# Keeping a block's query weights and a quarter of a K tile on chip, with five stream slots instead of six

## The chip, the cores and the metric

The kernel runs on one core of a Trainium2 chip. The metric is the time of one execution on the device in microseconds. The kernel before takes 1979.28 us, the median of 3 runs (1979.23 to 1979.42).

## The reference

One token goes through four attention layers: block A, block B, block A again, block B again, with the same weights and caches the second time. Each block has 32 heads, a cache of 8192 keys and values of 192 numbers per head, and a model width of 640.

```python
def block(x, k_cache, v_cache, wq, wo):          # x (1, 1, 640)
    q = (x @ wq).reshape(1, 1, 32, 192).transpose(0, 2, 1, 3)
    scores = jnp.einsum("bhqd,bhkd->bhqk", q, k_cache) * (192 ** -0.5)
    o = jnp.einsum("bhqk,bhkd->bhqd", softmax(scores), v_cache)
    return o.transpose(0, 2, 1, 3).reshape(1, 1, 32 * 192) @ wo

x = x + block(layernorm(x), A_k, A_v, A_wq, A_wo)
x = x + block(layernorm(x), B_k, B_v, B_wq, B_wo)
x = x + block(layernorm(x), A_k, A_v, A_wq, A_wo)
x = x + block(layernorm(x), B_k, B_v, B_wq, B_wo)
```

All inputs are bf16. Each cache holds 32 x 8192 x 192 numbers, 100.7 MB, so four layers read some 805 MB of keys and values unless a part of them is kept on chip.

## The kernel before

**Tiles and slots.** Layers count from 0 to 3; layers 0 and 2 use block A's tensors, layers 1 and 3 block B's. Heads are worked on in 16 pairs. A pair's K tile, and likewise its V tile, is 6144 KB: 128 partitions, 64 of them for each head, with 48 KB each. It is handled as two halves of 3072 KB, u = 0 and 1. On chip there is a pool of eight slots of 3072 KB (`NSLOT`, `TS`), each with a semaphore of its own (`semS`). Everything that is streamed passes through these slots: K tiles, V tiles, the query weights `wq` (7680 KB, two and a half slots) and the output weights `wo` in three parts a layer.

**One pair.** `products` lets DVE multiply the K tile by the broadcast query, in place, and PE sum the products by matmuls with an identity matrix (24 of them per half). `softmax` reduces and exponentiates, `values` multiplies the weights with the V tile on PE, `gather` picks out and stores the pair's output. The half u of a K tile is free again when its 24 matmuls are done, a V tile when its values are. After five pairs, `columns` and `project_row` or `project` bring the outputs through `wo`.

**Queries.** Layer l needs its whole query before it can work on more than one pair. The first pair's query comes from matmuls with a broadcast left side (L529), the others from `q_rows` (60 matmuls into one row each, which ScalarE then scales) and `q_spread` (one matmul per pair that broadcasts the row). In layers 0 and 1 the whole `wq` is loaded; the columns of the pair that comes first in layer l + 2 are copied to `wq0` by DVE (L522), so that the later layer loads only the other 15 pairs' columns, 7200 KB.

**What stays.** `KEPT` names the tiles that are loaded in layers 0 and 1 and still there two layers later: K tile 0 of block A (its products in layer 0 go to two other slots, steps `t`) and V tiles 14 and 15 of block B. Through layers 0 and 1 six slots are left for the stream, in layer 2 four once K tile 0 is used up.

**The queue.** SP issues all transfers in the order of `plan`. `allot` gives each transfer slots when the kernel is built: those that come free first. `before` lists what must be done with them, `freed` the events, `transfer` issues after a wait for these events. SP works strictly in order, so a transfer that waits for its slot holds up all behind it. A tile whose halves lie in neighbouring slots is loaded by one transfer (`whole`), which then needs both slots free and lands as a whole. In layers 0 and 1 this holds for K except pairs 5 and 10, and for V except the last.

**Between layers 1 and 2.** At the end of layer 1 four slots hold V tiles 14 and 15 and two hold K tile 0 of block A. In one of the other two lies the last part of `wo`. Layer 2 loads its query weights in five rows of 1440 KB (`r`, L405): two into the free slot, the third when a part of `wo` has been used (`woa`), the fourth when the projection has ended, the fifth when the first has been used. Meanwhile `quarter` works on K tile 0 in four pieces, and the slot halves that they release take the first V tile (`vh`, L426).

The places to have at hand: L405 issues the rows of query weights, L430 and L432 whole and half tiles, L434 the whole `wq`, L443 `wo`; L563 and L72 are matmuls of the query rows (L72 is a helper that also serves products and values); L675 and L705 are DVE's products; L690, L714 and L72 PE's sums; L645 ends the projection of layer 0.

Of the kernel before, what the change touches and what calls it, by code (L numbers as in the profile page):

```python
# [77 lines left out]
PAIRS_W = 5  # L78
NSLOT = 8
KEPT = {0: {("k", 0)}, 1: {("v", 14), ("v", 15)}}  # L80


def build(nc, A_x, A_k, A_v, A_wq, A_wo, B_x, B_k, B_v, B_wq, B_wo, out):
# [13 lines left out]
    QC = (NPAIR - 1) * PD  # L97
    QR = QC // 3
# [13 lines left out]
    with ExitStack() as ctx:  # L112
# [12 lines left out]
        wq0 = [sb(f"wq0{i}", [P, DC, PD], BF16) for i in range(2)]  # L125
# [103 lines left out]
        def whole(kind, l, p):  # L229

            if kind == "t":
                return False
            if kind == "k":
                return l < 2 and p not in (PAIRS_W, 2 * PAIRS_W) or l == 3 and p > 1
            if p == NPAIR - 1:
                return False
            return l != 2 or p not in (0, PAIRS_W, 2 * PAIRS_W)

        steps, plan = [], []
# [5 lines left out]
        for l in range(NL):  # L245
            if l < 2:
                plan.append(("wq", l, 0))
                steps += [("wq", l, g) for g in range(3)]
            elif l == 2:
                plan += [("wq", l, g) for g in range(3)]  # L250
                steps.append(("r", l, 0))
            else:
                both(("wq", l, 0))
            for p in range(NPAIR):
                if first_load("k", l, p) == (l, p):
                    plan += [("k", l, p, u) for u in range(2)]
                if stays("k", l, p):
                    plan += [("t", l, p, u) for u in range(2)]
                if l == 2 and p == 0:
                    for i, q in enumerate(("mr", "md", "mdrr", "mdd")):  # L260
                        for c in q:
                            steps.append({"m": ("mq", l, p, i), "r": ("r", l, sum(n[:2] == ("r", l) for n in steps)),
                                          "d": ("rd", l, p, sum(n[:2] == ("rd", l) for n in steps))}[c])
                        if i == 1:
                            steps.append(("r", l, 2))
                else:
                    steps.append(("m", l, p, 0))
                    if l == 2 and p == 1:
                        steps.append(("e", l, 0))
                    steps.append(("m", l, p, 1))  # L270
# [5 lines left out]
                if p < NPAIR - 2:  # L276
                    if first_load("v", l, p) == (l, p):
                        plan += [("v", l, p, u) for u in range(2)]
                        if l == 2 and p == 1:
                            i = plan.index(("k", l, 1, 0))  # L280
                            plan[i - 1:i + 1] = [("k", l, 1, 0), ("v", l, 0, 1)]
# [25 lines left out]
        def released(n):  # L307

            if n[0] in "kvt":
                l, p = n[1:3]  # L310
                if n[0] != "t" and stays(*n[:3]):
                    l, p = l + 2, ORDER[l + 2]["pairs"].index(pair(l, p))
                return at[("v", l, p, 1) if n[0] == "v" and p == NPAIR - 1 else ("v", l, p) if n[0] == "v" else
                          ("mq", l, p, 2 * n[3] + 1) if (l, p) == (2, 0) else ("m", l, p, n[3])]
            return at[("wol", n[1]) if n[0] == "wo" and n[2] == 2 and NB[n[1]] else ("r", 2, (0, 3, 4)[n[2]]) if n[:2] == ("wq", 2) else n]

        place, before, holder = {}, {}, [None] * NSLOT

        def allot(n):

            if n[0] == "wq" and n[1] < 2:
                ns = [("wq", n[1], g) for g in range(3)]
            elif n[0] == "v" and (n[2] < NPAIR - 1 or n[1] == 1) or n[0] == "k" and whole(*n[:3]):
                ns = [n[:3] + (u,) for u in range(2)]
            else:
                ns = [n]
            k = len(ns)
            end = [-1 if h is None else released(h) for h in holder]
            first = -1 if n[1] == 0 and n[0] == "k" and stays(*n[:3]) else 1
            i = min(range(0, NSLOT - k + 1, 2 if k == 2 else 1), key=lambda i: (max(end[i:i + k]), first * i))  # L330
            if n[:3] == ("v", 2, 0):
                i = place["k", 0, 0, 0]
            for j, m in enumerate(ns):
                place[m] = i + j
                before[m] = [h for h in holder[i:i + k] if h is not None]
                if n[0] in "kv" and not whole(*n[:3]):
                    before[m] = [h for h in holder[i + j:i + j + 1] if h is not None]
            for j, m in enumerate(ns):
                holder[i + j] = m

        for n in plan:
            if n[0] == "wol":
                before[n] = [] if NB[n[1]] else [("wc", n[1], 2)]
            elif n[0] in ("wob", "vq", "woe"):
                before[n] = []
            elif n not in place:
                allot(n)
        assert before["wq", 2, 1] == [("wo", 1, 2)] and before["wq", 2, 2] == [("wq", 2, 0)] and before["v", 2, 0, 0] == [("k", 0, 0, 0)]
        for g, (c0, k) in enumerate(Q_PARTS):
            i = plan.index(("wq", 2, g))  # L350
            plan[i:i + 1] = [("r", 2, c) for c in range(c0, c0 + k)]
            for c in range(c0, c0 + k):
                before["r", 2, c] = before["wq", 2, g]
        before["r", 2, 2], before["r", 2, 4], before["vh", 2, 0] = [("woa", 1, 2)], [("r", 2, 0)], [("kq", 2, 0, 0)]
        plan.insert(plan.index(("v", 2, 0, 0)), ("vh", 2, 0))
        turn = {}
        for i, n in list(enumerate(plan)):
            if n[0] == "v" and n[3] == 0:
                m = n[:3] + (1,)
                turn[n[1:3]] = (0, 1)  # L360
                if n[2] < NPAIR - 1 and not whole(*n[:3]) and max(map(released, before[n])) > max(map(released, before[m])):
# [6 lines left out]
        def wq_rows(l, g):  # L368

            c0, k = Q_PARTS[g]  # L370
            if l < 2:
                i = place[("wq", l, 0)] * TS
                return pool[:, i + c0 * QW:i + (c0 + k) * QW].rearrange("p (c n) -> p c n", c=k)
            return slot[place[("wq", l, g)]][:, 0:k * QC].rearrange("p (c n) -> p c n", c=k)
# [8 lines left out]
        def transfer(n):  # L383
# [10 lines left out]
            if n[0] == "t":  # L394
                return max(free, key=lambda e: e[1]) if free else None
# [6 lines left out]
            if n[0] == "r":  # L402
                g = n[2] // 2
                i = place["wq", 2, g]
                return SP.op(lambda s: s.dma_start(  # L405
                    wq_rows(l, g)[:, n[2] % 2, :],
                    w["wq"][:, o["q1"] * PD:o["q1"] * PD + QC].rearrange("(p c) n -> p c n", c=DC)[:, n[2], :]), *free,
                    sem=semR[g] if n[2] % 2 else semS[i], inc=16)
            if n[0] == "vq":
                n = ("v", l, NPAIR - 1, 1)  # L410
            first = n[0] == "vh"
            if first:
                n = ("v", l, 0, 0)
            i = place[n]
            t = slot[i]
            if n[0] in "kv":
# [7 lines left out]
                if n == ("v", 2, 0, 0):  # L424
                    x = slice(0, TS // 2) if first else slice(TS // 2, TS)
                    return SP.op(lambda s: s.dma_start(t[:, x], r[:, x]), *free, sem=semS[i], inc=16)  # L426
                if whole(*n[:3]):
                    if n[3] == 1:
                        return landed[n[:3] + (0,)]
                    f = lambda s: s.dma_start(pool[:, i * TS:(i + 2) * TS], r)  # L430
# [4 lines left out]
            elif n[0] == "wq":  # L435
# [3 lines left out]
                    w["wq"][:, o["q1"] * PD:o["q1"] * PD + QC].rearrange("(p c) n -> p c n", c=DC)[:, c0:c0 + k, :])  # L439
# [59 lines left out]
        def layer(l, ev_z, ev_true):  # L499
# [17 lines left out]
            PE.wait(ev_xb, last["QB"])  # L517
            if l < 2:
                e = need(("wq", l, 0))
                every = pool[:, place[("wq", l, 0)] * TS:][:, 0:DC * QW].rearrange("p (c n) -> p c n", c=DC)  # L520
                q0 = ORDER[l + 2]["q0"] * PD
                ev_first[l] = DV.op(lambda v: v.tensor_copy(wq0[l][:], every[:, :, q0:q0 + PD]), e)  # L522
                q_first = every[:, :, ORDER[l]["q0"] * PD:(ORDER[l]["q0"] + 1) * PD]
            else:
                e = ev_first[l - 2]
                q_first = wq0[l - 2]
            PE.wait(e)
            for c in range(DC):
                e = PE.op(lambda t, c=c: t.matmul(  # L529
                    QM[:, 0:PD], lhsT=xb[:, c:c + 1].broadcast_to([P, P]), rhs=q_first[:, c, :],  # L530
                    start=(c == 0), stop=(c == DC - 1)), signal=(c == DC - 1), bank=QMu)
# [13 lines left out]
            q_halves(0, e, ev_rs, scale=rs)  # L545

            def q_rows(g, r0=0, r1=None):
# [3 lines left out]
                t3 = wq_rows(l, g)[:, :, ORDER[l]["q1"] * PD if l < 2 else 0:]  # L551
                PE.wait(need(("wq", l, 0)) if l < 2 else need(("r", 2, c0 + r0) if l == 2 else n), ev_xb, last["O"],
                        last["YB"], ev_first.get(l))
                r1 = k if r1 is None else r1
                for c in range(r0, r1):
                    for b in range(4):
                        w = min(512, QR - b * 512)
                        for r in range(3):
                            fin = c0 + c == DC - 1
                            o, x, y = (OY[32 * r:32 * r + 1, b * 512:b * 512 + w], xb[:, c0 + c:c0 + c + 1],  # L560
# [399 lines left out]
```

## Time and profile before

| | |
|---|---|
| median of 3 runs | 1979.28 us |
| span of the profiled execution | 1977.8 us |
| read from HBM | 848.36 MB, 429 GB/s over the span |
| PE busy | 1267.5 us (64%) |
| DVE busy | 1198.7 us (61%) |
| ACT busy | 168.2 us (9%) |
| chain that ended last | DMA 58%, PE 25%, DVE 15% |
| DVE products L675 | 360 of 2392 ns mean, idle before them 151.0 us, released by DMA |
| layer 2's query weights | 5 transfers of 1440 KB |
| layer 3's query weights | 2 of 2880 KB, 1 of 1440 KB |

The profiled execution's span, from its first instruction to its last, is 1.5 us shorter than the median time. DMA's share counts all 16 DMA engines. KB are 1024 bytes, MB and GB/s are decimal. A transfer's landing is the time at which the last of its sixteen completions arrives, one for each DMA engine.

### The profile page before, as it was taken

The numbers are of one execution on the slowest core, as the hardware profiler recorded it, in microseconds if no ns is written. First come the engines' busy times: TensorE is split into PE (matmuls) and PEld (weight loads), VectorE is DVE, ScalarE is ACT, GpSimd is POOL, SyncE is SP. The second block draws the span as 40 slices with busy tenths as digits, with TensorE's granted clock in tenths as the row PEclk, the third lists the DMA queues.
The fourth block names the chain that finished last, engine by engine and source line by source line (L and its number), as shares of the span: only waits on it lengthen the run. The fifth ranks groups of instructions, "written<-read, shape, count | busy, mean of one in ns | idle before, by whom it ended". The sixth has DMA issues, their size and how long they took to land.

```text
span 1977.8 us, 12008 instructions
## 1 busy us (share of the span) xinstructions
PE 1267.5 (64%) x7742; PEld 127.0 (6%) x2599; DVE 1198.7 (61%) x812; ACT 168.2 (9%) x529; POOL 4.6 (0%) x24
## 2 busy tenths in 40 slices
PE   3567466566476566665786666666666667657668
PEld 0000000000100000000020000000001001000001
DVE  3567467467167656656756565665764765665756
ACT  0000000000000100100010000000000100000000
POOL 0000000000000000000000000000000000000000
PEclk9778787778677787777887777877787878777779
DMA  9999999999999999999999999999999999999998
GB/s 414 431 442 430 430 430 431 435 437 423 433 435 436 431 429 429 432 437 432 428 410 436 427 431 431 433 430 430 432 429 428 435 429 434 439 429 431 432 432 374
DMA packets 27095, 849.12 MB, mean 429 GB/s; under 512 B 3106, under 2 KB 3236, under 8 KB 3876
## 3 DMA queue, kind: packets, MB, share of 16 engines
q1 hardware_dynamic: 26900, 848.38, 99.7%
q8 instruction: 40, 0.66, 0.1%
q14 instruction: 11, 0.09, 0.0%
q10 hardware_dynamic: 144, 0.00, 0.0%
HBM read 848.36 MB, written 0.00 MB: 429 GB/s over the span
## 4 chain that ended last, share of the span: by engine, by line
DMA 58%; PE 25%; DVE 15%; ACT 1%; issue 1%; SPq 0%
DMA pool<-in_B_k_cache_dram 24%; DMA pool<-in_A_v_cache_dram 17%; DMA pool<-in_A_k_cache_dram 15%; PE S L72 14%; DVE pool L675 11%; PE OY L72 5%; PE OY L790 3%; DMA pool<-in_B_v_cache_dram 3%; DVE s_sb L733 1%; ACT p_sb L748 1%; DVE OY L814 1%; PE OY L628 1%; DVE acc L816 1%; PE S L690 1%; DVE m_bf L735 0%
## 5 line engine op out<-in xcount | busy, mean ns | idle before, releaser
L675 DVE TENSOR_TENSOR pool<-pool,q_sb 128x3072 bf16<-128x3072 bf16 (+1 forms) x360 | 837.6, 2392 | 151.0 <-DMA pool<-in_B_k_cache_dram 84.8
L72 PE MATMUL S<-pool,ident 128*128 128x512 bf16 x3004 | 782.9, 422 | 18.1 <-DVE pool L675 16.7
L814 DVE TENSOR_TENSOR OY<-OY,small 128x1536 f32<-128x1536 f32 x60 | 106.0, 1766 | 255.0 <-PE OY L72 254.9
L72 PE MATMUL OY<-pool,p_sb 128*16 128x512 bf16 x1920 | 206.0, 517 | 0.0
L828 PE MATMUL TB<-acc,small 128*33 128x192 f32 x120 | 46.3, 484 | 210.3 <-DVE acc L816 210.3
L733 DVE TENSOR_REDUCE s_sb<-S 128x128 f32<-128x1024 f32 x63 | 77.1, 1224 | 160.0 <-PE S L72 160.0
L690 PE MATMUL S<-pool,ident 128*128 128x512 bf16 x64 | 37.4, 584 | 212.4 <-DVE pool L675 212.3
L790 PE MATMUL OY<-pool,p_sb 128*16 128x512 bf16 (+1 forms) x1216 | 142.6, 490 | 45.3 <-DMA pool<-in_A_v_cache_dram 43.8
L542 ACT ACTIVATE q_sb<-QM 64x192 bf16<-64x192 f32 x120 | 38.9, 324 | 942.4 <-PE QM L580 941.7
L816 DVE TENSOR_REDUCE acc<-OY 128x192 f32<-128x1536 f32 x60 | 105.4, 1757 | 2.0
L837 ACT ACTIVATE rows<-TB,small 1x192 bf16<-1x192 f32 x120 | 49.5, 412 | 557.0 <-PE TB L828 555.5
L748 ACT ACTIVATE p_sb<-s_sb,small 64x128 bf16<-64x128 f32 x128 | 55.7, 435 | 172.1 <-DVE small L742 171.3
L804 DVE RECIPROCAL small<-TB 33x2 f32<-33x2 f32 x64 | 11.1, 173 | 94.3 <-PE TB L763 78.1
L738 PE MATMUL QM<-ident,m_bf 128*64 128x64 bf16 x128 | 14.0, 216 | 82.6 <-DVE m_bf L735 82.6
L763 PE MATMUL TB<-small,ones 128*33 128x2 f32 x120 | 14.4, 190 | 74.1 <-ACT p_sb L748 74.1
L580 PEld LDWEIGHTS QM<-rows,one_b 1*128 1x128 bf16 x60 | 5.5, 91 | 737.0 <-issue 731.0
L790 PEld LDWEIGHTS OY<-pool,p_sb 128*16 128x16 bf16 (+1 forms) x1216 | 34.6, 105 | 195.2 <-issue 138.5
L628 PE MATMUL OY<-pool,oT 128*1 128x320 bf16 x330 | 38.6, 411 | 2.2 <-ACT oT L658 2.2
L742 DVE TENSOR_REDUCE small<-QM 128x1 f32<-128x64 f32 x64 | 14.3, 224 | 27.8 <-PE QM L738 27.8
L828 PEld LDWEIGHTS TB<-acc,small 128*33 128x33 f32 x120 | 10.3, 133 | 297.9 <-DVE acc L816 292.0
L748 ACT ACTIVATION_READ_ACCUMULATOR p_sb<-s_sb,small 64x1 f32 x128 | 23.3, 182 | 0.0
L690 PEld LDWEIGHTS S<-pool,ident 128*128 128x128 bf16 x64 | 6.6, 103 | 249.8 <-DVE pool L675 246.8
(87 smaller groups left out, 245.2 us busy)
## 6 DMA issues: line engine op xcount, KB each, us to landing
pool<-in_B_k_cache_dram SPq DMA_DIRECT2D x28, 6144.0 KB, 35.8
pool<-in_B_v_cache_dram SPq DMA_DIRECT2D x28, 6144.0 KB, 31.0
pool<-in_A_v_cache_dram SPq DMA_DIRECT2D x27, 6144.0 KB, 26.9
pool<-in_A_k_cache_dram SPq DMA_DIRECT2D x34, 3072.0 KB, 20.4
pool<-in_A_k_cache_dram SPq DMA_DIRECT2D x14, 6144.0 KB, 34.8
pool<-in_A_v_cache_dram SPq DMA_DIRECT2D x9, 3072.0 KB, 13.8
pool<-in_B_k_cache_dram SPq DMA_DIRECT2D x8, 3072.0 KB, 22.4
pool<-in_A_wo_dram SPq DMA_DIRECT2D x6, 2400.0 KB, 20.9
```

Of the source, the lines that this page charges most:

```text
L72: return t.add_instruction(mybir.InstMatmult(name=t.bass.get_next_instruction_name(), engine=mybir.EngineType.PE, ins=[t.lower_ap(rhs), t. ...
L542: lambda a, h=h, r=r, f=f: a.activation(q_sb[i][r, :], QM[r, h * DH:(h + 1) * DH], ACT.Copy, scale=f),
L628: e = PE.op(lambda t, i=i, h=h, f=l < 3 and n[2] == 0 and i == 0, fin=n == last_row and i == k - 1: t.matmul(YR[32 * h:32 * h + 1, :], lhs ...
L675: e = DV.op(lambda v, d0=d0: v.tensor_tensor(k3[:, :, d0:d0 + QD], kin[:, :, d0:d0 + QD], q_sb[qi][:, d0:d0 + QD].unsqueeze(1).broadcast_t ...
L690: t.matmul(S[:, :], lhsT=ident[:], rhs=k3[:, :, d0:d0 + R], start=d0 == 0, stop=fin)),
L733: lambda v: v.tensor_reduce(s[:], S_[:].rearrange("p (j r) -> p j r", r=R), AX.X, ALU.add),
L748: ev_p[p] = AC.op(lambda a, h=h, r=r: a.activation(p_sb[par][r, :, h], s[r, :], ACT.Exp, bias=negm[par][r, 0:1], accum_out=l_col[par][r, h ...
L790: t.matmul(o, lhsT=x, rhs=y, start=f, stop=fin) if c == 0 else
L814: e = DV.op(lambda v: v.tensor_tensor(o3, o3, pick[:, 0:VK].unsqueeze(2).broadcast_to([P, VK, DH]), ALU.mult), bank=Ou)
L816: e = DV.op(lambda v: v.tensor_reduce(acc[:], O.rearrange("p (i d) -> p d i", d=DH), AX.X, ALU.add), e, bank=Ou)
L828: e = PE.op(lambda t: t.matmul(TB[64:97, C_O:C_O + DH], lhsT=half33, rhs=acc[:], start=True, stop=True), bank=TBu)
L837: last["TO"] = last["row_written"] = AC.op(lambda a, h=h: a.activation(orow[:, o0 + h * DH:o0 + (h + 1) * DH], TB[64 + 32 * h:65 + 32 * h, ...
```

## The change

`KEPT` no longer names a K tile of block A. In its place the whole query weights of block A stay in slots 5, 6 and the first half of 7 from layer 0 until layer 2 has used them (`A_WQ`), and the second half of slot 7 keeps the untouched first quarter of K tile 0 (`K0Q`). In layer 0 that quarter is loaded by a transfer of its own (`kh`) and multiplied from there into slot 0.

Through layers 0 and 1 the stream has slots 0 to 4. Which slots a transfer takes is written down in `RINGS`, one entry per transfer in the order of `plan`: two digits that follow one another mean one transfer into two neighbouring slots, which waits for both; others, such as `40` and `04`, mean two transfers of a half. `wq` of layer 1 goes to slots 2 to 4. Pairs 5 and 10 now come as whole K tiles; pairs 1, 7 and 13 have split K tiles and pairs 3, 9 and 10 split V tiles.

In layer 2 no query weights are loaded. Quarters 1 to 3 of K tile 0 are (`kq`), 1536 KB each, into the two halves of slot 4 and the first half of slot 5: after `woa`, after the whole projection, and after the first part of the query weights has been used. The next K tile takes slots 4 and 5, V tile 0 slots 6 and 7. The first query of layer 2 is formed from the weights in place, in two steps around the first part of the rows (`lead`).

`wq0` becomes one buffer with the columns of two pairs, filled in layer 1 by three copies; layer 3 forms the queries of its first two pairs from it (`LEAD`) and loads the other 14 pairs' columns, 6720 KB.

```diff
-KEPT = {0: {("k", 0)}, 1: {("v", 14), ("v", 15)}}
+KEPT = {0: set(), 1: {("v", 14), ("v", 15)}}
+RINGS = ["01 23 40 12 34 01 23 04 12 34 0 12 34 01 23 40 12 34 01 23 04 1 23 04 12 34 01 23 40 12 34 01 23 4 0 1",
+         "234 01 23 40 12 34 01 23 04 12 34 0 12 34 01 23 40 12 34 01 23 04 1 23 04 12 34 01 23 40 12 34 01 23 4 01"]
...
-    QC = (NPAIR - 1) * PD
-    QR = QC // 3
+    LEAD = [1, 1, 1, 2]
+    QC = [(NPAIR - n) * PD for n in LEAD]
+    QR = -(-(NPAIR - 1) // 3) * PD
...
-        wq0 = [sb(f"wq0{i}", [P, DC, PD], BF16) for i in range(2)]
+        wq0 = sb("wq0", [P, DC, LEAD[3] * PD], BF16)
+        A_WQ = NSLOT - 3
+        K0Q = slot[NSLOT - 1][:, TS // 2:]
+        QUARTER = [K0Q, slot[A_WQ - 1][:, 0:TS // 2], slot[A_WQ - 1][:, TS // 2:], slot[A_WQ][:, 0:TS // 2]]
...
-                plan += [("wq", l, g) for g in range(3)]
-                steps.append(("r", l, 0))
+                steps += [("lead", l, 0, 0), ("wq", l, 0), ("lead", l, 0, 1), ("wq", l, 1), ("wq", l, 2)]
...
+                if l == 2 and p == 0:
+                    plan += [("kq", l, p, i) for i in range(1, 4)]
...
+            if n[1] < 2:
+                slots = [int(i) for i in rings[n[1]].pop(0)]
+                halves = n[0] == "v" and n[2] == NPAIR - 1
+                if n[0] in "kv" and len(slots) == 2 and slots[1] == slots[0] + 1 and not halves:
+                    joint.add(n[:3])
+                put([n] if len(slots) == 1 else [n[:-1] + (u,) for u in range(len(slots))], slots, n[0] == "wq" or n[:3] in joint)
...
+            elif n[0] == "kq":
+                before[n] = [None, ("woa", 1, 2), ("wo", 1, 2), ("wq", 2, 0)][n[3]:n[3] + 1]
+                if n[3] == 3:
+                    put([("k", 2, 1, 0)], [A_WQ - 1])
+                    put([("k", 2, 1, 1), ("v", 2, 0, 0), ("v", 2, 0, 1)], [A_WQ, A_WQ + 1, A_WQ + 2])
+                    before["k", 2, 1, 0] = [("kq", 2, 0, 1), ("kq", 2, 0, 2)]
+                    before["k", 2, 1, 1] = [("kq", 2, 0, 3)]
+                    before["v", 2, 0, 1].append(("kq", 2, 0, 0))
...
-                ev_first[l] = DV.op(lambda v: v.tensor_copy(wq0[l][:], every[:, :, q0:q0 + PD]), e)
+            if l == 1:
+                q0 = (ORDER[3]["q0"] + 1 - LEAD[3]) * PD
+                for c0, k in Q_PARTS:
+                    ev_first[c0] = DV.op(lambda v, c0=c0, k=k: v.tensor_copy(
+                        wq0[:, c0:c0 + k, :], every[:, c0:c0 + k, q0:q0 + LEAD[3] * PD]), ev_all)
...
+            def q_lead(p, c0=0, c1=DC):
+                if l < 3:
+                    x, w, ev = pair(l, p) * PD, every, ev_all
+                else:
+                    x, w, ev = (pair(l, p) - ORDER[l]["q0"] - 1 + LEAD[l]) * PD, wq0, ev_first[Q_PARTS[-1][0]]
+                PE.wait(ev_xb, last["QB"], ev)
+                for c in range(c0, c1):
+                    e = PE.op(lambda t, c=c: t.matmul(
+                        QM[:, 0:PD], lhsT=xb[:, c:c + 1].broadcast_to([P, P]), rhs=w[:, c, x:x + PD],
+                        start=(c == 0), stop=(c == DC - 1)), signal=(c == c1 - 1), bank=QMu)
+                if c1 == DC:
+                    q_halves(p, e, ev_rs, scale=rs)
...
+                if (l, p, u) == (0, 0, 0):
+                    parts = [(K0Q.rearrange("p (j d) -> p j d", d=DH), k3[:, 0:JU // 2, :], JU // 2), (k3[:, JU // 2:, :],) * 2 + (JU // 2,)]
```

## The prediction

> **What bounds the kernel now.** I read the page first, then stretches, then the chain and the timeline where slots change hands.
>
> ```profile
> span 1977.8 us, 12008 instructions
> ...
> DMA  9999999999999999999999999999999999999998
> ...
> q1 hardware_dynamic: 26900, 848.38, 99.7%
> q8 instruction: 40, 0.66, 0.1%
> ```
>
> The transfer queue is busy for 99.7% of the span; PE (64%) and DVE (61%) have slack. The only spells without any packet are 1.75 us at the start and 2.5 us at the end. So the time is bytes over rate, plus whatever the queue starves. In mid-stream 6144 KB tiles land 14.53 us apart, and two 3072 KB halves 7.30 + 7.31: a tile split in two costs 0.07 us more.
>
> ```profile
> 300.00:500.00 200.00, 129.26 (x742) 11.20 (x225) 128.78 (x77) 16.89 (x56) 0.00 (x0) 0.77 1.00 431
> ...
> 1023.00:1026.00 3.00, 3.00 (x23) 0.10 (x1) 3.00 (x4) 0.00 (x0) 0.00 (x0) 1.00 0.96 363
> ...
> 1033.00:1035.00 2.00, 1.11 (x4) 0.19 (x2) 0.25 (x1) 1.48 (x3) 0.00 (x0) 0.89 0.98 332
> ...
> 1971.50:1973.50 2.00, 1.78 (x26) 0.74 (x13) 0.83 (x2) 0.00 (x0) 0.00 (x0) 1.00 0.52 209
> ```
>
> These are windows (length, busy time by engine, granted clock, DMA share, GB/s). Just before the end only half of the 16 DMA engines still work (share 0.52): they run apart. The trace keeps sixteen completions per transfer; first and last lie 0.5 us apart at the first tile, 3.0 at 508 us, 4.7 at 1011 us. Each of the 40 instruction fetches on q8 sets one engine back by some 1.45 us. The slowest engine counts, and the others' lead soaks up their own fetches. Near 1023 and 1033, where layer 2 begins, the leading engines do run dry (363 and 332 GB/s).
>
> ```profile
> 270.62 34.28 DMA pool<-in_A_k_cache_dram
> ...
> 304.93 3.37 DVE pool L675
> ...
> 308.35 0.61 PE S L690
> 308.95 12.88 PE S L72 x47
> ```
> ```profile
> 316.67 0.33 SPq L432 DMA_DIRECT2D pool<-in_A_k_cache_dram  x1
> ```
>
> In the chain, a K tile lands whole at 304.9, DVE multiplies, PE sums. Its first half is released at 316.64 (SP issues into it at once): 11.7 us after landing. That number decides the change.
>
> **The change, part by part.**
>
> *Bytes.* Layer 2 no longer loads five 1440 KB pieces of query weights (L405); they land between 1011.57 and 1028.88: −17.31 us. It loads three quarters of K tile 0, 1536 KB each, at 3.66 us (neighbours of that size land 3.65 to 3.70 apart): +10.98. Layer 3's weights shrink from 15 to 14 tile pairs, 480 of 7200 KB, whose pieces took 6.92 + 6.93 + 3.46 us: −1.15. The table splits six tiles per layer in layers 0 and 1 where two were split: eight more, +0.56. Together **−6.92 us**.
>
> *Layer 0 to 1.* The 7680 KB weights now wait for the output-weight slot too (slots 2, 3, 4), not only for the values before it:
>
> ```profile
> 498.25 0.43 SPq L434 DMA_DIRECT2D pool<-in_B_wq_dram  x1
> ...
> 504.75 1.98 PE L645 MATMUL OY<-ones,pool 1*64 1x1 f32 x20 [0.53 <-ACT pool L641]
> ```
>
> They go out at 506.76 instead of 498.25, and the slowest engine has emptied the queue by 507.49 (last landing 507.92 less 0.43, the lag at the end of the program). So I need the lead R that an issue needs not to starve an engine. The trace has no such wait on all engines, so bounds: in layer 2 one issue came 0.76 us before the leading engine ran out and lost it 1.10, R = 1.9; another 2.3 us before lost nothing; at program start the engines' first data imply 1.9 to 2.25. Right after a dry spell (the 332 GB/s row) R was 3.0 to 4.3. I take 1.9, the row most like a single dry spell. Then the loss is 506.76 + 1.9 − 507.49 = **+1.2** (0.9 at R 1.6, 2.3 at 3.0). Behind it on SP stands K tile 0, which was issued at 508.28 anyway.
>
> *Layer 1 to 2.* Before, two weight pieces could be queued early in a free slot. Now one slot is left; quarter 1 goes out at 1006.35 (the event of L405's third issue), quarter 2 only when the last projection ends:
>
> ```profile
> 1012.77 0.74 PE L594 MATMUL OY<-oTl,pool 128*128 128x1 bf16 x15
> ...
> 1017.03 0.59 PE L563 MATMUL OY<-pool,xb 128*1 128x512 bf16 x3
> ...
> 1017.41 0.80 PE L72 MATMUL OY<-pool,xb 128*1 128x512 bf16 x9
> ...
> 1022.98 3.93 SPq L426 DMA_DIRECT2D pool<-in_A_v_cache_dram  x2
> ```
>
> Quarter 1's data end at 1011.14 + 3.66 = 1014.80; quarter 2, issued 1013.54, is effective at 1015.44: +0.64. It ends near 1019.1. Quarter 3 waits for the first weight part: two leading matmuls (0.32 each) from 1015.29 and 24 rows matmuls (1.2 + 0.8) end near 1018.1, effective 1020.0 at R 1.9, 1021.1 at 3.0: +0.9 to 2.0, I take 1.3. V tile 0's first half follows with 24 more matmuls at 1020.9 and is in time. Together **+1.9** (1.2 to 2.6). All queued behind these on SP comes later by the same.
>
> *Five stream slots.* A whole K tile now needs the first half of the K tile before it, released m0 after its landing, and must be queued R before the V tile in between ends on the slowest engine, 14.53 − 0.43 = 14.1 us after the landing. The spare is s = 14.1 − R − m0. From the release times, m0 at the places where both tiles are whole is 10.68, 11.48, 10.91, 10.51 in layer 0 and 11.56, 10.64, 10.17, 10.77 in layer 1; four tiles that follow tiles now joined I set at 10.8 (estimate, the mean); four behind output weights depend on the second half instead, 10.29, 11.22, 10.93, 10.47 once the 5.7 us of that load are taken off. Sum of the sixteen 172.8. At R 1.9, s is 0.6 to 2.0, so the slowest engine is not stalled. But no engine can lead it by more than s, where leads were up to 4.7. A fetch on a follower then adds up to 1.45 − s to the end. About 20 fetches meet 16 such places: the positive parts of 1.45 − s add up to **+2.6** (R 1.6: 1.1; R 3.0: 18.4). V tiles wait for the values before, 22.1 to 25.4 us after landing, against 28.6 − R: spare 1.4 and more, next to nothing added.
>
> Of the Trainium skill, "DMA: Bandwidth & Descriptors" (Latency and other measured facts) gives 0.6 us to the first byte of such a transfer and, for HBM, 0.2 us on average but 2 us at high load. The trace had its first packet 1.0 us after the issue. With 0.6 + 2 = 2.6 us for R, an estimate from that page of the Trainium skill, this term would be 12 us; that latency itself no row here shows apart.
>
> *At nothing.* Layer 0's weight copy (L522, 1.15 us of DVE) goes; layer 1's becomes three, twice the elements, about 2.3 us, inside DVE's wait for K tile 0 (13.4 us). Leading queries from weights in place: five matmuls, 1.8 us, while tiles load. Quarter 0 of layer 2 starts some 2 us later behind the rows; the slots that it frees are wanted near 1029 and free near 1025. Layer 0's first K tile is read out of place in pieces, eight DVE operations for four; its slot is not wanted for another 10 us. Without cover each would cost its own length once.
>
> **Sum:** −6.92 + 1.2 + 1.9 + 2.6 = −1.2 on 1977.8. The profiled execution lies 1.5 us below the median of 1979.28 and I carry that over: **1978.1**.
>
> **Rivals.**
> (a) *The queue stays ahead.* Leading engines lost at most 0.1 us where an issue came 1.6 to 2.3 us ahead; against it stand the two boundaries, whose release times are fixed. With R 1.6 and no coupling between engines: −6.92 + 0.9 + 1.2 = −4.8, **1974.5**. Only this is faster.
> (b) *Starvation feeds itself, slower.* Engines that had just run dry needed 3.0 to 4.3 us. In layers 0 and 1 leading engines would be dry at each K tile, so that may be the rule. At R 2.5 the sixteen places cost 172.8 − 16 × 10.15 = 10.4, the boundaries 1.8 and 2.1: +7.4, **1986.7**. It passes the old time once R exceeds about 2.0, and +0.2% at about 2.3. Against it: a V half soon after the dry spell needed no more than 2.7. The Trainium skill's 2.6 (above) would belong to this case.
> (c) *The saved bytes are idle time anyway*, that is, layer 2's first quarters make compute the bound: its second K tile would be worked on 5 us earlier than before, while values and quarters end only 2 to 3 later; slots still come free about 5 us ahead. Price if wrong: the whole 6.9 on top of the sum, **1985.0**.
>
> **How the numbers follow.** 0.2% is 4.0 us, about what a measurement of this kernel can tell from no change. Forecast and its neighbourhood (1975.3 to 1983.2) 0.40, with R between 1.7 and 2.3; (a) 0.26; (b) 0.30; (c) 0.04. R is the unknown, and its bounds pull unequally, so the range runs from 1973.8, a little below (a), to 1989.0, above (b). The likeliest case alone spans 1975 to 1983. So faster 0.26, same 0.40, slower 0.34.
>
> **What would show it.** 845.2 MB read instead of 848.4. Dry spells of 1 to 2 us near 508 and 1015 to 1021. In layers 0 and 1 the sixteen completions of a tile within 2 us of each other, where they were 3 to 4.7 apart. If they still lie 3 or more apart, (a) is right. If K tiles land over 29.2 us apart again and again, with GB/s under 425 in the slices of layers 0 and 1, (b) is. A wait of DVE on quarters far longer than 3 us would show (c). The forecast is wrong outright if SP's K issues in these layers come later than 12 us after the landing.

## The result, and the profile after

The changed kernel takes 1996.77 us (median of five runs, 1992.41 to 2001.51), the kernel before 1979.41 beside it (1979.23 to 1979.99): 17.4 us slower, ratio 1.0084, 95% interval 1.0072 to 1.0097. That is above the range of the prediction, and on the side to which it gave 0.34. The profiled execution is one of the quicker ones (1993.56 us), 14.0 us longer than the one before by span. Two executions, of 2155.76 us (the repetition of the changed kernel) and of 2562.74 us (the first run of both repairs), were in a slow state and are left out of every median, ratio and range below.

These rows are from the page of the changed kernel: span, rate of the transfers in 40 slices, the queue of the stream, the bytes read.

```profile
span 1991.8 us, 12020 instructions
...
GB/s 411 436 415 422 419 428 423 427 430 427 405 429 421 426 423 432 419 425 426 425 381 433 433 428 432 435 428 427 440 423 427 435 436 433 428 439 429 430 438 365
...
q1 hardware_dynamic: 27764, 845.23, 99.2%
...
HBM read 845.22 MB, written 0.00 MB: 424 GB/s over the span
```

The rate in the same slices of the kernel before:

```profile
GB/s 414 431 442 430 430 430 431 435 437 423 433 435 436 431 429 429 432 437 432 428 410 436 427 431 431 433 430 430 432 429 428 435 429 434 439 429 431 432 432 374
```

The bytes went as announced (845.2 MB). The loss is in the rate, and in the first half of the span: slices 3 to 5 (415, 422, 419), 11 (405), 13 (421) and 17 (419) are low, slice 21, between layers 1 and 2, is 381 (410 before); from slice 22 on the row looks like the one before.

The chain of waits in the window 120 to 160 us of the changed kernel, start and length of each piece:

```profile
107.76 18.92 DMA pool<-in_A_k_cache_dram
126.68 0.02 issue
126.70 3.37 DVE pool L687
130.07 0.05 issue
130.12 0.61 PE S L702
130.73 7.52 PE S L72 x23
138.25 0.02 issue
138.26 17.95 DMA pool<-in_A_k_cache_dram
```

This is a closed loop: a K tile lands, DVE multiplies, PE sums its first half, and the end of that sum (11.57 us after the landing) lets the next K tile go out. In the kernel before such a transfer was issued 34.28 us ahead of its landing; here it is 18 to 19, of which 14.5 are its own bytes.

Windows of the changed kernel (length, busy time of PE, PEld, DVE, ACT and POOL, granted clock, DMA share, GB/s; a packet counts whole where it starts, so in a short window a share can come out above 1):

```profile
134.00:138.00 4.00, 4.00 (x16) 0.00 (x0) 4.00 (x2) 0.00 (x0) 0.00 (x0) 0.78 1.07 461
138.40:139.20 0.80, 0.80 (x6) 0.00 (x0) 0.80 (x1) 0.00 (x0) 0.00 (x0) 1.00 0.15 61
...
514.40:515.60 1.20, 1.20 (x19) 0.64 (x23) 0.00 (x0) 0.00 (x0) 0.00 (x0) 0.59 0.00 0
1036.80:1037.90 1.10, 1.10 (x15) 0.30 (x6) 0.00 (x0) 0.37 (x1) 0.00 (x0) 0.97 0.05 11
```

Right after the issue at 138.26 most engines have nothing to do (share 0.15); at the two boundaries between layers nearly none works for over 1 us.

From landing to landing (last of the sixteen completions), the profiled executions of both kernels and of the experiments below, each as its difference from the kernel before, in us (the last two columns are from the runs in more rounds):

| stretch | before | after | K in halves | query weights in two | waits alone, 12 places | waits alone, 20 | later wait | halves + two | + early quarters |
|---|---|---|---|---|---|---|---|---|---|
| layer 0, to its last output rows | 507.92 | +6.84 | +1.99 | +5.73 | +4.78 | +3.28 | +14.64 | +1.58 | +1.19 |
| to layer 1's query weights | 18.17 | +2.95 | +2.27 | +0.05 | -0.02 | -0.03 | -0.03 | +0.07 | +0.06 |
| layer 1, to its last output rows | 485.47 | +7.51 | +2.65 | +4.27 | +2.60 | +5.43 | +16.77 | +0.68 | +0.82 |
| layer 2, to its first output weights | 154.69 | -2.20 | -3.35 | -2.23 | +0.22 | +0.27 | -0.43 | -2.70 | -1.80 |
| to layer 2's last output rows | 334.66 | +0.40 | +0.06 | -0.59 | +0.28 | +0.26 | +0.38 | +0.36 | +0.41 |
| to layer 3's query weights | 32.28 | -1.50 | -1.25 | +0.06 | -0.35 | -0.34 | -0.36 | -1.52 | -1.46 |
| to the last landing | 441.65 | +0.03 | 0.00 | +0.03 | -0.10 | -0.07 | -0.04 | 0.00 | +0.11 |

For the changed kernel the column adds up to the 14.03. Layers 0 and 1, where the ring has five slots, cost 14.35 (6.84 and 7.51); the boundary to layer 1 costs 2.95; layer 2 with its boundary gains 2.20 and layer 3's weights 1.50.

Where in the layers? For each transfer I took the mean of its sixteen completions, less the time of its bytes at the usual rate. In layer 0 this mean falls back at the eight transfers that the prediction counted (K tiles of pairs 3 to 6 and 9 to 12): 0.91, 1.21, 0.99, 0.98, 0.75, 0.48, 0.66 and 0.81 us, 6.8 together. Besides, the first quarter of K tile 0, now a transfer of its own right at the start, loses 0.47 (0.25 to 0.45 in the other runs that have it); why isn't shown. In layer 1 it is nine of the K tiles, the eight counted ones and pair 8, and one V tile, 6.9 together. Every other transfer of the two layers, split ones included, loses under 0.3.

### The profile page after: what moved, and what is told of

The parts are those of the page before. It is cut to its first block, busy times and chain, and to the rows that moved or that the text cites. A ratio compares the mean times of both kernels' runs of the same rounds, so it can differ in the third digit from the quotient of the medians.

```text
span 1991.8 us, 12020 instructions
## 1 busy us (share of the span) xinstructions
PE 1286.6 (65%) x7741; PEld 129.5 (7%) x2601; DVE 1197.4 (60%) x817; ACT 168.6 (8%) x529; POOL 4.6 (0%) x24
## 4 chain that ended last, share of the span: by engine, by line
DMA 54%; PE 25%; DVE 19%; ACT 1%; issue 0%; SPq 0%; DVEq 0%
DMA pool<-in_B_k_cache_dram 22%; PE S L72 16%; DMA pool<-in_A_k_cache_dram 15%; DVE pool L687 14%; DMA pool<-in_A_v_cache_dram 14%; PE OY L72 4%; DMA pool<-in_B_v_cache_dram 3%; PE OY L799 2%; DVE OY L823 1%; DVE acc L825 1%; DVE s_sb L742 1%; PE S L702 1%; ACT p_sb L757 1%; PE OY L637 1%; DVE pool L716 1%
## 5 line engine op out<-in xcount | busy, mean ns | idle before, releaser
L687 DVE TENSOR_TENSOR pool<-pool,q_sb 128x3072 bf16<-128x3072 bf16 (+2 forms) x364 | 837.6, 2368 | 167.9 <-DMA pool<-in_B_k_cache_dram 87.2
L799 PE MATMUL OY<-pool,p_sb 128*16 128x512 bf16 (+1 forms) x1216 | 146.8, 506 | 36.1 <-DMA pool<-in_A_v_cache_dram 33.4
L772 PE MATMUL TB<-small,ones 128*33 128x2 f32 x120 | 14.5, 191 | 74.2 <-ACT p_sb L757 74.2
```

The lines of the kernel that those rows point to most:

```text
L687: e = DV.op(lambda v, d0=d0, kin=kin, kout=kout, n=n: v.tensor_tensor(kout[:, :, d0:d0 + QD], kin[:, :, d0:d0 + QD], q_sb[qi][:, d0:d0 + Q ...
L799: t.matmul(o, lhsT=x, rhs=y, start=f, stop=fin) if c == 0 else
```

## The experiments

The theory was that the lead is what was lost: a whole K tile is issued too shortly before the engines run out. The rival was that smaller transfers, the new ring or the boundaries cost the time. The kernel before, run beside each set, took 1979.4 to 1979.7.

**K tiles in halves.** In the changed kernel, no K tile but the first counts as joint any more; each half waits for its own slot.

```diff
-                if n[0] in "kv" and len(slots) == 2 and slots[1] == slots[0] + 1 and not halves:
+                if (n[0] == "v" or n[:3] == ("k", 0, 0)) and len(slots) == 2 and slots[1] == slots[0] + 1 and not halves:
```

> The changed kernel with every K tile of layers 0 and 1 but the first loaded as two 3072 KB transfers, each waiting only for its own slot; slots, bytes and order as in the changed kernel. Theory 'lead': the five-slot ring lost about 14.35 us in layers 0 and 1 because a whole K tile is issued only when the first half of the K tile before it is released, 2.5 to 4 us before the slowest engine runs dry, and at sixteen places the 16 engines lost 0.4 to 1.2 us each on the mean. Split, the first half waits for values that ended long ago and covers 7.3 us, so that loss goes; 24 more splits at 0.07 us add 1.7. Expected 1996.8 - 14.35 + 1.7 = 1984 us (1981 to 1987). Rival 'transfers': more, smaller transfers and the ring itself cost the time, not the wait: 1997 to 2000.

Measured 1982.26 us, ratio to the kernel before 1.0011 (1.0002 to 1.0021). No K or V tile of layers 0 and 1 loses 0.3 us any more (the first quarter at the start still loses 0.4), with the same slots, bytes and order, and with 25 transfers more; the two layers lose 4.64 us instead of 14.35. Transfers and ring as such are not the cause of the rest.

**Query weights in two.** Rows 0 to 3 wait for V tile 14 alone, row 4 for the output weights.

```diff
-                plan.append(("wq", l, 0))
+                plan += [("wq", l, 0), ("wqb", l)][:l + 1]
...
-        before["kh", 0, 0] = []
+        before["kh", 0, 0], before["wqb", 1] = [], [("wo", 0, 2)]
...
+        before["wq", 1, 0].remove(("wo", 0, 2))
```

> The changed kernel with the 7680 KB of layer 1's query weights loaded in two transfers: rows 0 to 3 (6144 KB) wait only for the values before, row 4 (1536 KB) for the output weights. Theory 'lead': the queue's dry spell of 1.30 us near 514 us goes, and with it the 2.95 us that this boundary lost more than in the kernel before; nothing else changes: 1993.9 us (1991 to 1997, the changed kernel itself scatters by 4). In the trace the weights land 18.2 us after the last output rows, as in the kernel before, not 21.1. Rival 'pulled together': the engines then enter layer 1 further apart and its sixteen-fold waits take the gain back: 1996 to 1998, layer 1 longer by the 2.95.

SP's issues around 504 us in this run, the last output rows, then the weights in two parts:

```profile
503.75 0.33 SPq L407 DMA_DIRECT2D rows<-in_A_wo_dram  x1
504.12 0.43 SPq L446 DMA_DIRECT2D pool<-in_B_wq_dram  x1
512.96 0.33 SPq L425 DMA_DIRECT2D pool<-in_B_wq_dram  x1
```

Measured 1989.0 us, ratio 1.0047 (1.0032 to 1.0062). The first part goes out 9.5 us before the rows land (513.65), the weights land 18.22 us after them, and the 2.95 is gone, as expected. The time fell by more than it (by 4 to 8 us beside the changed kernel's 1993.0 and 1996.8) and lies under the expected range: layers 0 and 1 lost 10.0 instead of 14.35 in the profiled executions. Layer 0 is the same program in both up to this point, so 1.1 of that is scatter; I can't tell how much of layer 1's 3.2 is.

**The waits alone.** The kernel before, with all its slots and transfers; only the waits of the smaller ring are added. Of the sixteen, twelve bind: pairs 6 and 11 follow a tile in halves here, whose first half is released early.

```diff
+        for l in range(2):
+            for p in (3, 4, 5, 6, 9, 10, 11, 12):
+                before["k", l, p, 0].append(("k", l, p - 1, int(p in (5, 10))))
```

> The kernel before, with eight slots and all its transfers as they were; only, in layers 0 and 1 the K tiles of pairs 3, 4, 6, 9, 11, 12 also wait until the first half of the K tile before is released, and those of pairs 5 and 10 until its second half is: the waits of the changed kernel's five-slot ring, without anything else of it. Theory 'lead': the waits alone make most of the 14.35 us: 1979.4 + 8 to 14 = 1987 to 1993. Rival 'transfers': a wait that ends 2.5 to 4 us before the queue runs dry costs nothing: 1979 to 1981.

And the same on DVE's product, which ends earlier:

```diff
-                last["q"][qi] = chunks[-1]
+                last["q"][qi] = freed["dv", l, p, u] = chunks[-1]
```

> The kernel before with the same sixteen added waits, but on DVE's last product of the half tile instead of PE's sum of it, some 3.5 us earlier, so that each transfer goes out 6 to 7.5 us before the slowest engine runs dry. Theory 'lead': 6 us and more are enough: 1979 to 1981.5. Rival 'any wait': that the queue is not filled far ahead costs by itself, whatever the lead: about the time of the run with the later wait, 1987 to 1993.

The chain of waits of the first of the two, and SP's issue of the same K tile in the second:

```profile
278.99 3.37 DVE pool L678
282.36 0.05 issue
282.41 0.61 PE S L693
283.02 6.50 PE S L72 x23
289.52 0.02 issue
289.54 19.91 DMA pool<-in_A_k_cache_dram
```
```profile
282.51 0.33 SPq L433 DMA_DIRECT2D pool<-in_A_k_cache_dram  x1
```

With the wait on the sum: 1988.34 us, ratio 1.0043 (1.0028 to 1.0058); the tile shown goes out 10.57 us after the landing of the one before (278.97). With the wait on the product: 1979.68, ratio 1.0001 (0.9992 to 1.0010); the same tile goes out 6.68 us after that landing (275.83 in this run). A wait without any of the rest of the change makes a good part of the loss, and the same wait with enough lead costs nothing.

**A lead in between, and the changed kernel once more.** The same waits in the kernel before, now on the seventh of the last twelve sums.

```diff
-                            signal=fin, bank=Su[u], holds=ident)
+                            signal=fin or c == NC - 1 and r == QD // R // 2, bank=Su[u], holds=ident)
+                        if c == NC - 1 and r == QD // R // 2:
+                            freed["mid", l, p, u] = e
```

> The kernel before with the same sixteen added waits, on an event between the two tried: the seventh of the last twelve sums of the half tile, some 1.4 us before its release, so that a transfer goes out about 4.5 us before the slowest engine runs dry (3.2 in the run that cost 8.7 us, over 6 in the one that cost nothing). Theory 'lead': an engine that still works needs 3.0 to 3.3 us, so 4.5 covers all but those that a fetch has just set back, and only leading engines more than 2.5 ahead run dry: 1980 to 1983. Rival 'in proportion': the loss goes with the missing lead, half of 8.7: 1984 to 1985.

> The changed kernel once more, beside the others of this set: 1993 to 2000 us (its runs so far scatter from 1992.4 to 2001.5). Theory 'lead' expects the same sixteen places to lose, with amounts that differ from execution to execution, because it depends on which DMA engine an instruction fetch has just set back; so layer 0 ends some 5 to 7.5 us later than in the kernel before, not always by the 6.84 of its first profile. Rival 'fixed cost': the same 6.8 within 0.5.

The lead in between took 1982.25 us, ratio 1.0013 (1.0004 to 1.0023): it cost 2.6 us, where the full delay cost 8.7. In the traces the slowest engine's lead at the twelve places was 4.3 us on the mean, against 3.5 with the full delay and 7.1 with the wait on the product; so the event came 0.9 us earlier, not the 1.4 that I had reckoned, and the loss falls faster than in proportion all the same. The changed kernel took 1993.03 (three executions, 1991.84 to 1994.98), ratio 1.0069 (1.0053 to 1.0086); its layer 0 was 8.15 us longer than before by the last completion, where the first profile showed 6.84. That lies beyond the 7.5 I had expected at most, and speaks against a fixed cost.

**More places, and a later wait.** First pairs 2, 3, 4, 7, 8, 9, 12 and 13 (with 5 and 10 as above), so that twenty places bind; then sixteen places that wait for DVE's last product of the second half. The lines are those of the second run.

```diff
+        for l in range(2):
+            for p in (2, 3, 4, 7, 8, 9, 12, 13):
+                before["k", l, p, 0].append(("dv", l, p - 1, 1))
```

> The kernel before with the waits alone, at twenty places that bind instead of twelve: in layers 0 and 1 the K tiles of pairs 2, 3, 4, 7, 8, 9, 12 and 13 wait for the first half of the K tile before, those of pairs 5 and 10 for its second half. (In the first run with such waits pairs 6 and 11 follow a tile in halves, which is released early, so that twelve of sixteen bound; the mean engine lost 4.24 and 3.91 us in the two layers, 0.68 a place.) Theory 'lead': the loss goes with the number of places, 20 x 0.68 = 13.6 us: 1990 to 1995, the changed kernel's time without anything else of it. Rival 'saturates': once the engines are pulled together, further places have little left to lose: 1987 to 1990.

> The kernel before with the wait at sixteen places (pairs 2, 3, 4, 7, 8, 9, 12, 13 of layers 0 and 1) made later: DVE's last product of the second half of the K tile before, 13.2 us after its landing, so that the transfer goes out some 0.7 us before the slowest engine runs dry. It weighs what an engine needs. Theory 'a working engine needs 3.0': 2.3 us at each place, 37 in all, and about 10 for fetches that nothing absorbs any more (8 of 16 stretches with one, some 1.3 each): 2020 to 2032. Rival '1.9 for every engine', the value of the prediction: 16 x 1.2 = 19 and the same 10: 2005 to 2012.

Twenty places: 1998.27 us, ratio 1.0099 (1.0083 to 1.0114), above what I expected, and with runs from 1988.33 to 2001.26. The profiled one was the quickest, with 8.7 us lost in layers 0 and 1, 0.44 a place; the median execution of the four was 18.8 us over the kernel before, about twice that. So the waits alone can cost as much as the changed kernel lost, but the amount per place isn't a constant, and the rival that it saturates is refuted by the median and not by the quickest execution.

The later wait took 2011.21 us (two executions, 2010.43 and 2011.99), ratio 1.0159 (1.0140 to 1.0177). Its chain and the window over the middle of layer 0:

```profile
97.58 13.17 DVE pool L678 x4
110.75 0.02 issue
110.77 18.09 DMA pool<-in_A_k_cache_dram
128.85 0.02 issue
128.88 13.18 DVE pool L678 x4
```
```profile
200.00:480.00 280.00, 167.49 (x972) 12.85 (x261) 164.26 (x92) 22.29 (x73) 0.00 (x0) 0.77 0.98 419
```

Here my theory of that moment fell. It said that a working engine needs 3.0 us and put the run at 2020 to 2032; the prediction's own 1.9 put it at 2005 to 2012, and that is where it came out, near the upper end. With a lead of 0.91 us for the slowest engine, that engine lost 1.14 to 1.39 us at the places without a fetch near, so it needed 2.05 to 2.3; the mean engine needed 1.72 to 1.97. So near a dry queue the R of the prediction was about right.

**What a lead is worth, engine by engine.** The packet records show why 1.9 holds there and yet fails at a lead of 3. A 48 KB packet takes 1.81 us when the queue is full, and packets of one engine follow each other without a gap, so that a trace can be sorted into sixteen rows. Three of them after the issue at 138.26 in the changed kernel (start+length, sorted in this way by me):

```
135.12+0.91 136.03+0.91 136.93+0.91 137.84+0.91 |             139.30+2.45 141.75+1.81
135.93+0.91 136.84+0.92 137.75+0.92 138.66+0.92 |             139.57+2.34 141.91+1.82
137.19+0.91 138.10+0.92 139.01+0.91 139.92+0.92 |             140.84+2.37 143.21+1.81
```

The first engine was dry at 138.75 and starts again 1.04 us after the issue; which of the restarts is its own the trace doesn't tell, as thirteen engines were dry by then and restarted between 139.23 and 139.72. The other two have no gap. But the first packet of all three takes 0.5 to 0.65 us longer than 1.81, even of the one that had 2.6 us of work left. Over layers 0 and 1 of 14 profiled executions (those of the table, their repetitions, and the runs with other leads), sorted by how long an engine still had work when the next transfer was issued (the rows from -0.5 to 0 and from 3.5 to 4 are not shown):

| lead of the engine, us | cases | idle before, us | first packet longer by, us | loss, mean | loss, 95th percentile |
|---|---|---|---|---|---|
| -1.0 to -0.5 | 139 | 1.80 | 0.70 | 2.50 | 3.00 |
| 0 to 0.5 | 174 | 0.84 | 0.68 | 1.52 | 2.02 |
| 0.5 to 1 | 321 | 0.46 | 0.59 | 1.05 | 1.52 |
| 1 to 1.5 | 365 | 0.19 | 0.50 | 0.69 | 1.54 |
| 1.5 to 2 | 359 | 0.17 | 0.29 | 0.46 | 1.98 |
| 2 to 2.5 | 377 | 0.10 | 0.21 | 0.31 | 1.58 |
| 2.5 to 3 | 504 | 0.07 | 0.13 | 0.19 | 1.30 |
| 3 to 3.5 | 483 | 0.01 | 0.05 | 0.06 | 0.35 |
| 4 and more | over 18,000 | 0.00 | 0.01 | 0.01 | 0.02 |

There is no step at 1.9. Up to a lead of 1.5 an engine loses on the mean 1.75 to 1.95 less its lead; from there to a lead of 3 a tail remains, in which one engine in twenty loses 1.3 to 2 us or more. At a gated place, one of those at which the K tile waits for the K tile before, the slowest engine had 2.5 to 4 us, but the leading ones 0 to 2.4.

**Both repairs.** K tiles in halves at the gated places only, and the query weights in two; then also the two late quarters of layer 2 earlier (layer 1's last output rows in the tile that layer 0 uses, the second part of its output weights projected before the last gather, quarter 3 behind one row of query weights instead of two).

```diff
-                if n[0] in "kv" and len(slots) == 2 and slots[1] == slots[0] + 1 and not halves:
+                if (n[0] == "v" or n[2] not in (3, 4, 5, 6, 9, 10, 11, 12)) and len(slots) == 2 and slots[1] == slots[0] + 1 and not halves:
```
```diff
-                steps.append(("e", l, p))
+                steps += [("e", l, p)] * (l == 3)
                 both(("wob", l))
+                steps += [("e", l, p)] * (l == 1)
...
-                before[n] = [] if NB[n[1]] else [("wc", n[1], 2)]
+                before[n] = [] if n[1] == 3 else [("wc", n[1], 2)]
...
-                before[n] = [None, ("woa", 1, 2), ("wo", 1, 2), ("wq", 2, 0)][n[3]:n[3] + 1]
+                before[n] = [None, ("woa", 1, 2), ("wo", 1, 2), ("row", 2, 0)][n[3]:n[3] + 1]
```

> The changed kernel with K tiles split only where a whole one would wait on the K tile before (pairs 3 to 6 and 9 to 12 of layers 0 and 1), and with layer 1's query weights in two transfers as in the boundary run. Theory 'lead': the run with all K tiles split came to 1982.3; the boundary gives back 2.3 (last engine) to 3.9 (mean engine) and eight splits less 0.6, so 1978 to 1979.5, about the kernel before. Rival 'pulled together': the boundary only pulls the engines together, and later waits take it back: 1981 to 1982.

> The run before, with the two late quarters of layer 2's first K tile released earlier: layer 1's last output rows go into the tile that layer 0 uses for its own, so quarter 2 waits for the second part of the output weights, which is projected before the last gather, some 2 us earlier; quarter 3 waits for the first of two rows of query weights, 1.8 us earlier. Theory 'lead': of the 2.15 and 2.25 us that the mean engine lost at these two quarters, quarter 2's goes and quarter 3 still loses 1 to 2: 1.5 to 2.5 us less than the run before, 1976 to 1978, under the kernel before. Rival: the chain of work between the layers, not the queue, sets the time there: no change.

> The kernel with split K tiles at the gated places and split query weights, in more rounds: 1978.1 as before (1977.5 to 1979); 0.5 to 2 us under the kernel before.

> The same with the earlier quarters, in more rounds: 1977.5 (1976.5 to 1978.5). In its first profile the quarters lost 3.3 us of the mean engine instead of 4.4, and layer 2 took 0.7 of it back, so 0.4 us under the run beside it is what is left to see.

With both repairs 1978.05 us, and 1977.73 in more rounds, ratio 0.9991 (0.9982 to 1.0000). With the earlier quarters 1977.55 and 1977.10, ratio 0.9990 (0.9981 to 0.9999). The second is 2.3 us under the kernel before, which its interval barely separates from none, and 16 to 20 under the changed one as it was. The page of the second, in more rounds:

```profile
span 1977.0 us, 12038 instructions
...
GB/s 414 430 428 434 434 428 431 429 436 428 435 432 426 435 427 434 428 431 435 426 385 436 428 422 432 432 431 431 433 427 429 437 427 434 432 435 432 432 431 370
...
q1 hardware_dynamic: 30212, 845.23, 99.6%
```

Slices 3 to 20 are back at 426 to 436; slice 21, the boundary between layers 1 and 2, is still 385. In the first profile of the version with earlier quarters the transfers of that boundary cost the mean engine 3.3 us, against 4.4 without; quarter 3 still lost 2.3, which I had put at 1 to 2. In the profiles of the further rounds the two versions lost the same there, 4.3 us: what quarter 2 gave back, the V half behind quarter 3 lost. The gain between the two versions, 0.5 and 0.6 us where I had expected 1.5 to 2.5, is too small for their scatter to be called shown.

## Why the prediction was wrong

**What bounds the kernel** was right: the stream. Every repair that gave the queue its lead back brought the time back, and none made an engine's work shorter.

**Bytes, -6.92: about right.** Layer 3's smaller weights gave 1.50 us by the last completion and 1.13 by the mean engine, predicted 1.15. In layer 2 the mean engine gained 3.52 up to the first output weights; its two late quarters lost 4.40 there, and the kernel before 1.58 at its first three V and K pieces (0.47, 0.35, 0.76), so the bytes gave 6.3, as predicted (6.33). The splits cost next to nothing, as said.

**Layer 0 to 1, +1.2: 2.95.** R was near (1.97 for the mean engine, 2.56 for the last). What failed is the release time: I put the issue at 506.76, 1.16 us before the last output rows land; it came at 514.76, just at that landing: the release was 8.0 us later than in the kernel before, the queue 6.84. That is 1.16 of the 1.75 missing; the rest is the slowest engine's larger need.

**Layer 1 to 2, +1.9: about 2.9** by the last engine (0.64 at quarter 2 and 2.23 at quarter 3, predicted 0.64 and 1.3). Here too R held and the release time did not: quarter 3 went out 5.92 us after quarter 2 (1031.01 and 1036.93) instead of 4.6. The 24 matmuls of the query rows that it waits for were put at 2.0 us, and took 3.3 (1033.53 to 1036.83) at a granted clock of 0.50.

**Five stream slots, +2.6: 14.35** (0.5 of it is the first quarter's own transfer at the start, which the prediction didn't price). This is the step that failed: the loss at the sixteen places was sized by a threshold for the slowest engine, and only fetches could cost anything. The runs showed starvation at each place instead: the mean engine fell back by 0.4 to 1.2 us at eight transfers of layer 0 and ten of layer 1, 13.7 together. That is what rival (b) foretold, "leading engines would be dry at each K tile", at more than its price; its reason, that engines which had just run dry need 3.0 to 4.3 us, didn't show (1.72 to 2.3 in the run with the later wait).

The release times behind the term were right: the K tiles went out 10.3 to 11.8 us after the landing of the K tile before, as predicted (behind output weights with the 5.7 us of that load taken off), and the losses lie at the predicted places and two more. Two things in the working were wrong. First, R was a threshold for the slowest engine: "so the slowest engine is not stalled". The runs show a slope with a tail, and slowest engines with a lead of 2.6 us lost 0.4 at 156 and 310 us, with no fetch near. Second, "A fetch on a follower then adds up to 1.45 − s to the end" supposes that the follower stood at the full lead s. It does so only just before a place. There the leading engines run dry and all restart nearer together (at 222.20 the completions came within 1.7 us, within 3.1 at the tile before). My reading is that the next fetch then finds an engine with next to no lead and goes to the end almost whole.

A sorting of the traces fits this: at the twenty transfers of layers 0 and 1 that were being moved when a fetch came, the last completion fell back by 15.3 us in the changed kernel's first profile and 12.1 in its second, against 4.2 in the kernel before; at all others but layer 1's query weights by 2.7 and 5.4, against 0.6. With R = 3.0 the prediction's formula would have given 18.4 for this term, nearer to the truth, but the later wait shows that 3.0 isn't what an engine needs: the number would have been nearer for a wrong reason.

**At nothing** held but for the first quarter's 0.5 us: no wait of DVE on layer 2's quarters replaced the saved bytes, so (c) is out.

**The signs** were well chosen. The 845.2 MB, the dry spells at 514 and 1036 us, and slices under 425 with K tiles up to 30.3 us apart were there. The spread of the completions, 0.7 to 3.1 us in layer 0, lay on both sides of the bound that the prediction set, and decided nothing. SP's K issues at these places came at most 11.8 us after the landing, or 16 to 17 at the four behind output weights, whose 5.7 us the prediction had taken off. By these signs (b) could be read off the first page.

**The first packet.** An engine that was dry at the issue started its first packet 1.07 us after it (median of the run with the later wait), and that packet took 0.69 us more than a full queue's. The Trainium skill, in "DMA: Bandwidth & Descriptors" (Latency and other measured facts), gives 0.6 us to the first byte. The 2.6 that the prediction estimated from that page of the Trainium skill is over what the dry engines needed (1.7 to 2.0); that the 12 us which it gave for this term came closer to 14.35 than the prediction's own 2.6 is luck, as with R = 3.0.

**Open:** how much of the 14 in a median run is the fetches' passing to the end and how much the tail of slow first packets. The sorting above leans to the fetches for the last engine, but it is no test: no run kept fetches away. Why a first packet is longer at a lead of 2 us isn't shown either.

## What to carry to other kernels

A stream on many parallel engines has no single lead: ask what each of the engines has left when the next transfer is issued, and price the leading ones, not only the slowest. Here 4 us of queued work per engine cost nothing, 3 us for the slowest cost 0.4 to 1.2 at every place, and the price is paid at each place. The likely reason, argued and not tested, is that running dry together takes away the spread that hides later disturbances. A transfer that waits for two slots waits for the later one; if the earlier can be filled first, splitting it costs 0.07 us here and buys half a tile's time of lead.

## What the runs showed that was not expected

Scatter came with the starved queue: the kernel before stays within 3.3 us over 25 runs, the changed one spreads over 9.7 in eight and the waits alone at twenty places over 13 in four. A loss that depends on which engine a fetch has just set back would do that; no run tested it, and the two executions with the later wait lie only 1.6 apart. And the first packet after an issue is longer by 0.5 to 0.7 us also on engines that never ran dry, up to a lead of some 1.5 us; a look for gaps alone misses more than half of the loss (in the changed kernel's first profile, by the same sorting into rows, the gaps make 4.2 us of the mean engine's loss in layers 0 and 1 and the longer first packets 8.3).
